# Four single PSUM tiles in place of two double ones in the joint keys of a packed attention and channel mix

## The chip, the cores and the metric

The kernel runs on one core of one Trainium2 chip. The metric is device time in microseconds (us), the median of several runs; lower is better. All profiles are of one execution on that core.

## What is computed

The reference is a two-step packed attention over eight batches, followed by a gated channel mix. Cut to what matters:

```python
p_packed = sm_attn(p, k, v)                # 32 packed rows per head
out      = sm_attn(q, p_packed, p_packed)  # (8, 8, 576, 64)
x        = out as (8, 576, 512)            # x_prev: x one row later, zeros first
xk = mu_k * x + (1 - mu_k) * x_prev
xr = mu_r * x + (1 - mu_r) * x_prev
k  = max(xk @ w_k, 0)                      # 512 -> 1024, the "keys"
v  = (k * k) @ w_v                         # 1024 -> 512, the "values"
r  = sigmoid(xr @ w_r)                     # 512 -> 512, the "gates"
return r * v
```

## The kernel before

The 4608 rows of the channel mix are cut into nine blocks of 512. Each fp32 product is made of three fp32r matmuls (high by high, high by low, low by high), so three matmuls of 128x128 by 128x512 form one step over a contraction of 128. The attention of later batches runs beside the channel mix of earlier blocks.

A planner written in the kernel (class `Flow`) runs generators, one for each piece of work, keeps the time at which each engine and each buffer slot should be free, and emits the instructions in the order in which it would start them. That order is fixed in the program: each engine takes its instructions in it, one after the other. Where an instruction needs what another engine makes, or overwrites what another engine still reads, the tile framework puts a semaphore wait on it. The framework keeps these dependences by tile.

The eight PSUM banks of 2 KB per partition are shared as follows. The tiles `m0` to `m3` have one bank each and serve keys, gates and values. The tiles `pa0` and `pa1`, made by `banks(slot)` (L276), have two banks each, shape 128 x 2 x 512, and serve attention.

The last two blocks (`PAIR` and `PAIR + 1`, blocks 7 and 8) have gates of their own (L1141 to L1143), and then their keys are made together (`keys_of_pair`, L1305 to L1341): seven products in place of eight, in the manner of Strassen and Winograd, each of two contraction steps of 128, so of six matmuls (all at L1334). There are two turns. In each turn a product is made for two column blocks `j` = 0 and 1 (`t` = 2 * turn + j). The order of the products is 1, 6, 7, 5, 2, 4, 3 in the first turn and 1, 6, 7, 5, 4, 3, 2 in the second. Products 1 and 6 open a `pa` tile for both `j`, products 7 and 5 open an `m` tile for each `j`; products 2, 4 and 3 add to the banks of 1, 7 and 5:

```python
FIRST_OF, WAITS = {2: 1, 4: 7, 3: 5}, {2: "u", 4: "x", 3: "c22"}
```

After each product a reader empties the bank: `first_of` copies product 1 to SBUF on ScalarE (ACT, L1355, result `c`, event `u`); `second_of` adds the bank of product 6 to it on VectorE (DVE, through `added`, L1195, event `v`); `third_of` adds product 7 (event `x`), `fourth_of` product 5 (`c22`), `low_left` product 4, `top_right` product 3, and `top_left` takes the relu of product 2 on ACT (L1385). Relu, square and the split into high and low follow (L1388 to L1426). `leave` gives a bank back to the planner, a double one after both its halves were read. Behind the joint keys come the values of the two blocks (L1170 to L1172), and then the gates' product with them (L1181) and the output's DMA (L242).

Of the kernel before, what the change touches and what calls it, by code (L numbers as in the profile page):

```python
# [8 lines left out]
F32 = mybir.dt.float32  # L9
# [173 lines left out]
def attn_pack_channel_mix(ctx: ExitStack, tc: tile.TileContext, q, k, v, p, mu_k, mu_r, w_k, w_v, w_r, out):  # L183
# [4 lines left out]
    P = 128  # L188
# [14 lines left out]
    flow = Flow()  # L203
# [33 lines left out]
    def pe(us, after=None):  # L237
        return "tensor", us, after, None
# [13 lines left out]
    def reached():  # L252
# [8 lines left out]
    sb = ctx.enter_context(tc.tile_pool(name="sb", bufs=1))  # L261
    dram = ctx.enter_context(tc.tile_pool(name="dram", bufs=1, space=bass.MemoryType.DRAM))
    ps = ctx.enter_context(tc.tile_pool(name="ps", bufs=1, space=bass.MemoryType.PSUM))
    BUFS = dict(raw=3, kq=4, vt=2, pt=1, a0=1, a1=1, aT=1, pm=2, e=2, a2=1, xt=4, tmp=4, xk=NC, sq=NF, sig=4,
                pa=2, both=1, m=4, staged=4, ex=7)
    for tag, n in BUFS.items():
        flow.pool(tag, n)
    flow.slots["m"].pop()
# [5 lines left out]
    MORE = {("sig", 4 + j): f"ex{3 + j}" for j in range(4)}  # L274

    def banks(slot):  # L276
        return ps.tile([P, 2, 512], F32, name="pa", tag=f"pa{slot}")

# [174 lines left out]
    def transposed_on_pe(tag, b, pr, raw_space, raw_slot, raw):  # L455

        yield from reached()
        kq = yield from flow.take("kq")
        t = tile_([P, S], F32, "kq", kq, tag)
        slot = yield from flow.take("pa")  # L460
        pT = banks(slot)
        yield pe(0.66)
        for hf in range(2):
            for c in range(3):
                nc.tensor.transpose(pT[:, hf, c * T6:(c + 1) * T6], raw[:T6, 3 * hf + c], ident[:T6, :T6])
        flow.give(raw_space, raw_slot)
        if b == 0 and pr < RANK_LATE14:
            done = flow.t
            yield vec(HS)
            nc.vector.tensor_copy(t[:, :HS], pT[:, 0, :HS])  # L470
            one = flow.t
            yield act(HS, after=done)
            nc.scalar.copy(t[:, HS:], pT[:, 1, :HS])
            flow.now.t = max(flow.t, one)
        else:
            yield act(S)
            nc.scalar.copy(t.rearrange("p (a b) -> p a b", a=2), pT[:, :, :HS])
        flow.give("pa", slot)
        ts[tag, b, pr] = kq, t
        flow.set((tag, b, pr))  # L480
# [68 lines left out]
    def first_side(h):  # L549
# [3 lines left out]
        slot = yield from flow.take("pa")  # L553
        yield pe(1.3)
        s1 = banks(slot)
        for hf in range(2):
            for j, half in enumerate(HALVES):
# [50 lines left out]
        slot = yield from flow.take("pa")  # L608
        yield pe(1.6)
        s2 = banks(slot).rearrange("p a b -> p (a b)")  # L610
        for k, (at, _) in enumerate(CHUNKS):
            for j in range(2):
# [690 lines left out]
    FIRST_OF, WAITS = {2: 1, 4: 7, 3: 5}, {2: "u", 4: "x", 3: "c22"}  # L1303

    def keys_of_pair():  # L1305
        left = [NF]
        for turn, order in enumerate(((1, 6, 7, 5, 2, 4, 3), (1, 6, 7, 5, 4, 3, 2))):
            opened, rooms = {}, {}
            for n in order:
                name, weights_ = PRODUCTS[n]  # L1310
                if n in (1, 6):
                    slot = yield from flow.take("pa")
                    both = banks(slot)
                    users = [2]
                for j in range(2):
                    t = 2 * turn + j
                    fs = slice(t * P, (t + 1) * P)
                    if n in (1, 6):
                        opened[n, j] = "pa", slot, both[:, j, :], users
                    elif n in (5, 7):  # L1320
                        one = yield from flow.take("m")
                        opened[n, j] = "m", one, ps.tile([P, 512], F32, name="ph", tag=f"m{one}"), [1]
                    more = n in FIRST_OF
                    bank = opened[FIRST_OF.get(n, n), j]
                    if more:
                        yield from flow.wait((WAITS[n], t))
                    for k in range(2):
                        yield from flow.wait(("difference", name, k), *([] if n in (1, 2, 4) else [("sum", {3: 4, 5: 1, 6: 2, 7: 3}[n], k)]))
                        yield pe(0.683)
                        flow.now.t -= flow.LAG  # L1330
                        wh, wl = weights_(k)
                        space, slot_, xh, xl = differences[name, k]
                        for step, (w, x) in enumerate(((wh, xh), (wh, xl), (wl, xh))):
                            nc.tensor.matmul(  # L1334
                                bank[2], w[:, fs], x, start=(not more and step == k == 0), stop=(step == 2 and k == 1),
                                skip_group_check=True,
                            )
                        if turn and j and space != "wk":
                            flow.give(space, slot_)
                    after = {1: first_of, 6: second_of, 7: third_of, 5: fourth_of, 2: top_left, 4: low_left, 3: top_right}[n]  # L1340
                    flow.spawn(after(turn, t, bank, rooms, left), 0, flow.t + flow.LAG)  # L1341

    def leave(bank):
        space, slot, _, users = bank
        users[0] -= 1
        if not users[0]:
            flow.give(space, slot)

    def first_of(turn, t, bank, rooms, left):
        space = "vt" if turn else "sq"  # L1350
# [7 lines left out]
    def second_of(turn, t, bank, rooms, left):  # L1358
        yield from flow.wait(("u", t))
        yield from added(rooms[t][1], rooms[t][1], bank[2])  # L1360
        leave(bank)
        flow.set(("v", t))
# [12 lines left out]
    def top_right(turn, t, bank, rooms, left):  # L1375
        yield from flow.wait(("c21", t))
        yield from added(rooms[t][1], rooms[t][1], bank[2])
        leave(bank)
        yield from later_square(t, rooms[t], rooms[t][1])

    def top_left(turn, t, bank, rooms, left):
        sr = yield from flow.take("tmp")
        r = tile_([P, WP], F32, "tmp", sr, "r")
        yield act(TB)
        nc.scalar.activation(r, bank[2], AF.Relu)  # L1385
        leave(bank)
        yield act(TB)
        nc.scalar.activation(r, r, AF.Square)  # L1388
        yield from squares_parted(PAIR, t, r, left)
        flow.give("tmp", sr)  # L1390
# [39 lines left out]
    def channel_mix():  # L1430
        for i in range(PAIR):
            yield from gates(i)
            yield from keys(i)
            if i + 1 < PAIR:
                mixes(i + 1)
            else:
                for h in range(2):
                    flow.spawn(mix(PAIR + h, 2, xrs, "xr"), 1 + 0.05 * h)
                flow.spawn(differences_of_keys(), 1.1)
            yield from values(i)  # L1440
        for h in range(2):
            yield from gates(PAIR + h)
        yield from keys_of_pair()
        for h in range(2):
            yield from values(PAIR + h, (0, 1, 4, 5, 6, 7, 2, 3))
# [91 lines left out]
```

## Time and profile before

| what | value |
|---|---|
| median of 3 runs | 587.63 us (587.18 to 588.07) |
| the profiled execution's own time | 586.58 us |
| its span, first to last instruction | 584.8 us |
| TensorE (PE) busy | 572.8 us, 98% of the span |
| VectorE (DVE) busy | 395.1 us, 68% |
| ScalarE (ACT) busy | 325.6 us, 56% |
| joint keys on PE | from 492.71 to 537.27 us |
| mean granted TensorE clock | 0.999 |

The busy time of PE counts overlapping matmuls once; two of them follow each other at a distance of some 0.23 us, and each is shown with 0.39 us. Idle time in a row stands in brackets with the instruction that ended it. So the cost of a gap is read from the distance between starts, and not from the bracket alone.

### The profile page before, as it was taken

How to read it: one execution, taken by the hardware profiler on the slowest of the kernel's cores; microseconds unless marked ns; L12 is line 12 of the kernel's file. 1: busy time of each engine (PE TensorE's matmuls, PEld its weight loads, DVE VectorE, ACT ScalarE, POOL GpSimd, SP SyncE). 2: the span in 40 equal slices, each digit the busy share in tenths (PEclk: the TensorE clock that was granted, in tenths of full speed). 3: DMA queues.
4: the chain of work that ended last, by engine and by line, in shares of the span. 5: the costliest groups of instructions: out<-in, count | busy, mean ns of one | idle time of the engine just before them, and what ended most of it. 6: DMA issues, size and time to landing. Idle time of an engine off the chain costs nothing.

```text
span 584.8 us, 9860 instructions
## 1 busy us (share of the span) xinstructions
PE 572.8 (98%) x3722; PEld 447.7 (77%) x3722; DVE 395.1 (68%) x745; ACT 325.6 (56%) x572; POOL 7.3 (1%) x36
## 2 busy tenths in 40 slices
PE   8999999999999999999999999999999999889997
PEld 7867777877777777777777777778888887667885
DVE  3797799739697688557953994479575992454531
ACT  3789979335576591665643764268456764346000
POOL 4000000000000000000000000000000000000000
PEclk9999999999999999999999999999999999999999
DMA  9899857646665542863375435000100010000011
GB/s 220 269 248 276 188 101 140 170 94 128 122 154 122 93 116 53 188 138 76 67 184 101 106 59 173 1 1 0 73 2 1 1 72 1 0 1 1 1 73 72
DMA packets 173823, 56.75 MB, mean 97 GB/s; under 512 B 150600, under 2 KB 164944, under 8 KB 173776
## 3 DMA queue, kind: packets, MB, share of 16 engines
q1 hardware_dynamic: 172928, 55.80, 40.5%
q8 instruction: 29, 0.48, 0.4%
q0 software_dynamic: 256, 0.26, 0.2%
q10 hardware_dynamic: 592, 0.07, 0.1%
q14 instruction: 18, 0.15, 0.1%
HBM read 43.13 MB, written 12.98 MB: 96 GB/s over the span
## 4 chain that ended last, share of the span: by engine, by line
PE 80%; DVE 7%; ACT 5%; DMA 4%; SPq 2%; issue 1%; POOL 0%; DVEq 0%; ACTq 0%; POOLq 0%
PE pvo L1170 10%; PE pvo L1171 9%; PE pvo L1172 9%; PE ph L1074 8%; PE ph L1076 7%; PE ph L1075 7%; PE pr L1141 5%; PE pr L1142 5%; PE pr L1143 5%; PE ph L1334 4%; PE pa L1334 3%; SPq L242 2%; DVE x L1041 2%; DMA st<-in_moe_w_r 2%; PE pa L914 2%; PE pa L742 1%
## 5 line engine op out<-in xcount | busy, mean ns | idle before, releaser
L1170 PE MATMUL pvo<-wv_h,sq 128*128 128x512 f32 x288 | 114.0, 396 | 0.2 <-ACT r L1086 0.2
L1171 PE MATMUL pvo<-wv_l,sq 128*128 128x512 f32 x288 | 112.2, 390 | 0.0
L1172 PE MATMUL pvo<-wv_h,sq 128*128 128x512 f32 x288 | 112.1, 389 | 0.0
L1074 PE MATMUL ph<-xk,wk_h 128*128 128x512 f32 x224 | 89.4, 399 | 0.0
L1075 PE MATMUL ph<-xk,wk_h 128*128 128x512 f32 x224 | 87.3, 390 | 0.0
L1076 PE MATMUL ph<-xk,wk_l 128*128 128x512 f32 x224 | 87.3, 390 | 0.0
L1170 PEld LDWEIGHTS pvo<-wv_h,sq 128*128 128x128 f32 x288 | 54.1, 188 | 17.9 <-issue 6.3
L1086 ACT ACTIVATE r<-ph 128x512 f32<-128x512 f32 x56 | 33.5, 598 | 61.2 <-PE ph L1076 57.8
L1172 PEld LDWEIGHTS pvo<-wv_h,sq 128*128 128x128 f32 x288 | 54.1, 188 | 11.4
L1171 PEld LDWEIGHTS pvo<-wv_l,sq 128*128 128x128 f32 x288 | 54.1, 188 | 10.6
L1041 DVE SCALAR_TENSOR_TENSOR x<-xt,mus,x 128x64 f32<-128x64 f32 (+7 forms) x117 | 52.7, 491 | 4.6 <-ACT x L1037 4.4
L1037 ACT ACTIVATE x<-xt,mus 128x64 f32<-128x64 f32 (+7 forms) x117 | 53.8, 514 | 1.2 <-DVE sq L1095 0.9
L1074 PEld LDWEIGHTS ph<-xk,wk_h 128*128 128x128 f32 x224 | 42.0, 188 | 13.1 <-issue 4.1
L1093 DVE CAST sq<-r 128x512 fp32r<-128x512 f32 x56 | 23.3, 417 | 42.4 <-ACT r L1089 41.1
L1141 PE MATMUL pr<-wr_h,xr 128*128 128x512 f32 x128 | 50.5, 395 | 0.0
L1142 PE MATMUL pr<-wr_l,xr 128*128 128x512 f32 x128 | 49.9, 390 | 0.0
L1143 PE MATMUL pr<-wr_h,xr 128*128 128x512 f32 x128 | 49.8, 389 | 0.0
L1076 PEld LDWEIGHTS ph<-xk,wk_l 128*128 128x128 f32 x224 | 42.0, 188 | 9.0
L1075 PEld LDWEIGHTS ph<-xk,wk_h 128*128 128x128 f32 x224 | 42.1, 188 | 8.0
L937 ACT COPY xt<-pa 128x576 f32<-128x576 f32 x28 | 33.3, 1254 | 14.2 <-PE pa L914 14.0
L1181 DVE TENSOR_TENSOR sig<-pvo,sig 128x512 f32<-128x512 f32 x36 | 23.3, 681 | 23.0 <-PE pvo L1172 22.9
L1095 DVE TENSOR_TENSOR sq<-r,sq 128x512 fp32r<-128x512 f32 x56 | 38.0, 679 | 1.0
(182 smaller groups left out, 849.7 us busy)
## 6 DMA issues: line engine op xcount, KB each, us to landing
out<-sig SPq DMA_DIRECT2D x36, 256.0 KB, 2.1
raw<-in_k SPq DMA_DIRECT2D x112, 72.0 KB, 2.7
raw<-in_q SPq DMA_DIRECT2D x112, 72.0 KB, 2.7
st<-in_moe_w_k SPq DMA_DIRECT2D x8, 512.0 KB, 5.8
st<-in_moe_w_v SPq DMA_DIRECT2D x8, 512.0 KB, 5.6
vt<-in_v SPq DMA_DIRECT2D x24, 160.0 KB, 3.4
away<-blocks SPq DMA_DIRECT2D x12, 288.0 KB, 2.7
vt<-in_v SPq DMA_DIRECT2D x24, 128.0 KB, 3.7
```

Source lines behind the costliest of these rows:

```text
L1037: nc.scalar.mul(x32[:, o:o + n], xts[b, c][:, 1 + s:1 + s + n], mus[:, j, c:c + 1])
L1041: nc.vector.scalar_tensor_tensor(x32[:, o:o + n], xts[b, c][:, s:s + n], mus[:, j + 1, c:c + 1], x32[:, o:o + n], op0=ALU.mult, op1=ALU.add,)
L1074: nc.tensor.matmul(ph, wk_h[:, c, fs], xh, start=(c == 0), stop=False)
L1075: nc.tensor.matmul(ph, wk_h[:, c, fs], xl, start=False, stop=False)
L1076: nc.tensor.matmul(ph, wk_l[:, c, fs], xh, start=False, stop=(c == NC - 1))
L1141: nc.tensor.matmul(pr, xh[:, ts_], wr_h[:, c, :], start=(c == 0), stop=False)
L1142: nc.tensor.matmul(pr, xh[:, ts_], wr_l[:, c, :], start=False, stop=False)
L1143: nc.tensor.matmul(pr, xl[:, ts_], wr_h[:, c, :], start=False, stop=(c == NC - 1))
L1170: nc.tensor.matmul(pv[t], sh, wv_h[:, f, :], start=(n == 0), stop=False)
L1171: nc.tensor.matmul(pv[t], sh, wv_l[:, f, :], start=False, stop=False)
L1172: nc.tensor.matmul(pv[t], sl, wv_h[:, f, :], start=False, stop=(n == NF - 1))
L1334: nc.tensor.matmul(bank[2], w[:, fs], x, start=(not more and step == k == 0), stop=(step == 2 and k == 1), skip_group_check=True,)
```

## The change

In `keys_of_pair` the four banks are taken one by one. The two `pa` tiles move to a pool of their own (`pp`), which is closed when the joint keys begin; a new pool (`late`) over the same four banks holds the tiles `n0` to `n3`, one bank each. Every product that opens a bank now opens one for its `j`, from slot kind `n` for products 1 and 6, and from `m` for 7 and 5, and `leave` gives back that bank alone.

```diff
+    pairs = ctx.enter_context(ExitStack())
+    pp = pairs.enter_context(tc.tile_pool(name="pp", bufs=1, space=bass.MemoryType.PSUM))
...
-                pa=2, both=1, m=4, staged=4, ex=7)
+                pa=2, both=1, m=4, n=4, staged=4, ex=7)
...
     def banks(slot):
-        return ps.tile([P, 2, 512], F32, name="pa", tag=f"pa{slot}")
+        return pp.tile([P, 2, 512], F32, name="pa", tag=f"pa{slot}")
...
     def keys_of_pair():
         left = [NF]
+        pairs.close()
+        late = ctx.enter_context(tc.tile_pool(name="late", bufs=1, space=bass.MemoryType.PSUM))
...
-                if n in (1, 6):
-                    slot = yield from flow.take("pa")
-                    both = banks(slot)
-                    users = [2]
                 for j in range(2):
                     t = 2 * turn + j
                     fs = slice(t * P, (t + 1) * P)
-                    if n in (1, 6):
-                        opened[n, j] = "pa", slot, both[:, j, :], users
-                    elif n in (5, 7):
-                        one = yield from flow.take("m")
-                        opened[n, j] = "m", one, ps.tile([P, 512], F32, name="ph", tag=f"m{one}"), [1]
+                    if n not in FIRST_OF:
+                        space = "m" if n in (5, 7) else "n"
+                        slot = yield from flow.take(space)
+                        opened[n, j] = space, slot, (ps if space == "m" else late).tile(
+                            [P, 512], F32, name="ph", tag=f"{space}{slot}"
+                        )
...
     def leave(bank):
-        space, slot, _, users = bank
-        users[0] -= 1
-        if not users[0]:
-            flow.give(space, slot)
+        flow.give(*bank[:2])
```

Every engine has the same instructions in the same order as before, by operation and operands; what changes is the tiles that L1334 (now L1335) writes, and the waits on its matmuls. In the rows below a number is part of a tile's name, and a wait names the engine whose semaphore is awaited.

On PE, the first turn, product 1 (moving tile `dB11`) and the start of product 6 (`dT2`), before:

```order
L1334 MATMUL pa_5319<-dB11_5185,wk_l_127 128x512
L1334 MATMUL pa_5319<-dB11_5000,wk_h_126 128x512 x2
L1334 MATMUL pa_5319<-dB11_5000,wk_l_127 128x512
L1334 MATMUL pa_5319<-dB11_5185,wk_h_126 128x512 [waits Activation_49]
L1334 MATMUL pa_5319<-dB11_5185,wk_h_126 128x512
L1334 MATMUL pa_5319<-dB11_5185,wk_l_127 128x512
L1334 MATMUL pa_5336<-dT2_5092,s2_4733 128x512 [waits PE_49]
L1334 MATMUL pa_5336<-dT2_5092,s2_4733 128x512
L1334 MATMUL pa_5336<-dT2_5092,s2_4734 128x512
L1334 MATMUL pa_5336<-dT2_5263,s2_4839 128x512
L1334 MATMUL pa_5336<-dT2_5263,s2_4839 128x512 [waits DVE_49]
```

The same place in the changed kernel:

```order
L1335 MATMUL ph_5326<-dB11_5188,wk_l_130 128x512
L1335 MATMUL ph_5335<-dB11_5003,wk_h_129 128x512 x2
L1335 MATMUL ph_5335<-dB11_5003,wk_l_130 128x512
L1335 MATMUL ph_5335<-dB11_5188,wk_h_129 128x512 x2
L1335 MATMUL ph_5335<-dB11_5188,wk_l_130 128x512
L1335 MATMUL ph_5344<-dT2_5095,s2_4736 128x512 x2
L1335 MATMUL ph_5344<-dT2_5095,s2_4737 128x512
L1335 MATMUL ph_5344<-dT2_5266,s2_4842 128x512 [waits Activation_49]
L1335 MATMUL ph_5344<-dT2_5266,s2_4842 128x512 [waits DVE_49]
L1335 MATMUL ph_5344<-dT2_5266,s2_4843 128x512
```

Before, the second half of product 1 (`j` = 1) is in the tile of the first half, and its second step waits for ACT. In the changed kernel it has a tile of its own and no wait; a wait on ACT stands at product 6 instead, on the matmul that first takes the second half of `dT2`.

On PE, the second turn, the end of product 6 and the start of product 7 (`dT3`), before:

```order
L1334 MATMUL pa_5471<-dT2_5092,s2_4733 128x512 x2
L1334 MATMUL pa_5471<-dT2_5092,s2_4734 128x512
L1334 MATMUL pa_5471<-dT2_5263,s2_4839 128x512 [waits DVE_49]
L1334 MATMUL pa_5471<-dT2_5263,s2_4839 128x512
L1334 MATMUL pa_5471<-dT2_5263,s2_4840 128x512
L1334 MATMUL ph_5487<-dT3_5051,s3_4714 128x512 x2
L1334 MATMUL ph_5487<-dT3_5051,s3_4715 128x512
```

The same place in the changed kernel:

```order
L1335 MATMUL ph_5490<-dT2_5095,s2_4736 128x512 [waits Activation_49]
L1335 MATMUL ph_5490<-dT2_5095,s2_4736 128x512
L1335 MATMUL ph_5490<-dT2_5095,s2_4737 128x512
L1335 MATMUL ph_5490<-dT2_5266,s2_4842 128x512 x2
L1335 MATMUL ph_5490<-dT2_5266,s2_4842 128x512
L1335 MATMUL ph_5498<-dT3_5054,s3_4717 128x512 [waits DVE_49]
L1335 MATMUL ph_5498<-dT3_5054,s3_4717 128x512
```

The wait on DVE in the middle of the second half of product 6 is gone. The first matmul into each bank that is opened again has a wait on the reader of what the bank held: ACT for product 6, whose bank held product 2, and DVE for product 7, whose bank held product 4.

On PE, the first turn, the end of product 2 (`dB21`) and the start of product 4 (`dT4`), before:

```order
L1334 MATMUL pa_5319<-dB21_5184,wk_h_126 128x512 x2
L1334 MATMUL pa_5319<-dB21_5184,wk_l_127 128x512
L1334 MATMUL pa_5319<-dB21_5264,wk_h_126 128x512 [waits Activation_49]
L1334 MATMUL pa_5319<-dB21_5264,wk_h_126 128x512
L1334 MATMUL pa_5319<-dB21_5264,wk_l_127 128x512
L1334 MATMUL ph_5351<-dT4_5198,wk_h_126 128x512 [waits DVE_49]
```

The same place in the changed kernel:

```order
L1335 MATMUL ph_5335<-dB21_5187,wk_h_129 128x512 [waits Activation_49]
L1335 MATMUL ph_5335<-dB21_5187,wk_h_129 128x512
L1335 MATMUL ph_5335<-dB21_5187,wk_l_130 128x512
L1335 MATMUL ph_5335<-dB21_5267,wk_h_129 128x512 x2
L1335 MATMUL ph_5335<-dB21_5267,wk_l_130 128x512
L1335 MATMUL ph_5360<-dT4_5201,wk_h_129 128x512 [waits DVE_49]
```

The wait on ACT stood in the middle of the second half's six matmuls; in the changed kernel it stands at their start, on the copy of product 1 out of this bank.

## Rows read from the trace of the kernel before

**Rows 1.** The page: busy time by engine, and the granted clock in 40 slices.
```profile
PE 572.8 (98%) x3722; PEld 447.7 (77%) x3722; DVE 395.1 (68%) x745; ACT 325.6 (56%) x572; POOL 7.3 (1%) x36
...
PEclk9999999999999999999999999999999999999999
```

**Rows 2.** Waits of PE over the whole span: us in total, times, longest us.
```profile
PE pa L1334 <- DVE c L1195: 1.7, 2, 0.9
...
PE pa L1334 <- ACT r L1385: 1.4, 2, 0.7
PE pa L1334 <- ACT c L1355: 1.4, 2, 0.7
```

**Rows 3.** The chain in order of time, joint keys: start, us, engine, tile, line.
```profile
494.95 0.59 ACT c L1355
...
498.71 0.70 DVE c L1195
...
500.42 5.45 PE ph L1334 x24
...
507.99 0.61 ACT r L1385
...
517.20 0.59 ACT c L1355
...
520.97 0.70 DVE c L1195
...
535.82 0.60 ACT r L1385
```

**Rows 4.** Timeline of PE at gaps: start, us, line, operation, tiles, [idle before].
```profile
494.52 0.39 PE L1334 MATMUL pa<-dB,wk_l 128*128 128x512 f32 x1
495.59 0.73 PE L1334 MATMUL pa<-dB,wk_h 128*128 128x512 f32 x2 [0.68 <-ACT c L1355]
496.16 0.40 PE L1334 MATMUL pa<-dB,wk_l 128*128 128x512 f32 x1
496.39 2.21 PE L1334 MATMUL pa<-dT,s 128*128 128x512 f32 x9
499.45 0.73 PE L1334 MATMUL pa<-dT,s 128*128 128x512 f32 x2 [0.85 <-DVE c L1195]
...
500.26 0.85 PE L1334 MATMUL ph<-dT,s 128*128 128x512 f32 x3
...
535.39 0.39 PE L1334 MATMUL pa<-dB,wk_l 128*128 128x512 f32 x1
536.47 0.72 PE L1334 MATMUL pa<-dB,wk_h 128*128 128x512 f32 x2 [0.69 <-ACT r L1385]
...
537.27 0.40 PE L1170 MATMUL pvo<-wv_h,sq 128*128 128x512 f32 x1
```

**Rows 5.** Windows: length, busy time (instructions) of PE, PEld, DVE, ACT, POOL; clock; DMA.
```profile
508.64:517.84 9.20, 8.52 (x36) 6.68 (x36) 6.78 (x12) 7.16 (x13) 0.00 (x0) 1.00 0.00 0
...
492.71:537.27 44.56, 40.14 (x170) 31.07 (x169) 18.78 (x30) 20.96 (x35) 0.00 (x0) 1.00 0.00 1
```

**Rows 6.** Tile pa from 400 us: the last instructions of attention that read it.
```profile
L937 ACT COPY xt<-pa x4: 1227/1237/1298, 405.6 to 410.8; 128x576 f32<-128x576 f32 x4
```

**Rows 7.** Timeline of DVE and PE: readers of banks, and products 4 and 3.
```profile
501.83 0.69 DVE L1195 TENSOR_TENSOR c<-c,ph 128x512 f32<-128x512 f32 x1 [0.61 <-PE ph L1334]
...
524.11 0.69 DVE L1195 TENSOR_TENSOR c<-c,ph 128x512 f32<-128x512 f32 x1 [0.63 <-PE ph L1334]
...
526.84 0.69 DVE L1195 TENSOR_TENSOR c<-c,ph 128x512 f32<-128x512 f32 x1 [0.67 <-PE ph L1334]
...
533.74 0.69 DVE L1195 TENSOR_TENSOR c<-c,ph 128x512 f32<-128x512 f32 x1
...
528.00 0.63 PE L1334 MATMUL ph<-dT,wk_h 128*128 128x512 f32 x2
...
530.80 2.90 PE L1334 MATMUL ph<-dB,s 128*128 128x512 f32 x12
```

## The prediction

> **What bounds the kernel now.** I read the page first: TensorE (PE) is busy 98% of the span, at full clock in every slice [rows 1]. So time can only come from work taken off PE or from gaps in its stream. Next I read PE's waits over the whole span: three of the four largest entries, two waits each, belong to L1334, the joint keys of the last two blocks: for a VectorE (DVE) add at L1195, a ScalarE (ACT) relu at L1385 and an ACT copy at L1355 [rows 2]. Then the chain of work that ended last, in order of time: inside the joint keys it leaves PE six times, for those same readers, and returns to PE each time [rows 3]. Six such detours, and each lies on the chain that sets the end: what is saved there is saved from the kernel's time, unless something else takes over. Last I read PE's timeline at the gaps, to price them [rows 4].
>
> **Why PE waits.** Look at the first gap. The row at 494.52 is the third matmul of `j` = 1 in product 1, so the last one of `j` = 0 began three steps earlier, at 493.84, and was over at 494.23. The copy of `j` = 0 starts only at 494.95, right after the matmul of 494.52 is over (494.52 + 0.39 = 494.91) [rows 3, 4]. Then PE waits until that copy is over and resumes at 495.59. Both halves lie in different banks, but in one tile: the copy waits for what was written to the other half, and the next matmul into the other half waits for the copy. The wait that PE has there is the one on ACT that stands in the middle of the second half's six matmuls. The contrast is in the same stage: products 7 and 5 have a tile for each `j`, their readers are DVE adds too, and 24 matmuls of theirs run through without a gap in 5.45 us, 0.227 us apart [rows 3]; the add that reads product 7 begins at 501.83 while PE goes on [rows 7].
>
> **What the change takes away.** With a tile for each `j`, neither half waits for the other. Price of one gap, from start to start, against 0.227 a step [rows 4]:
> - ACT kind: from 494.52 to 496.16 are three steps, 0.68, and it took 1.64: 0.96 lost. At the end of the second turn, from 535.39 to 537.27 are four steps, 0.91, and it took 1.88: 0.97. There are four of this kind (copies of product 1 and relus of product 2, two turns); the two not shown there have the same idle time within 0.01.
> - DVE kind (product 6, two turns): nine matmuls begin at 496.39 and take 2.21, so the ninth begins at 496.39 + 2.21 - 0.39 = 498.21; the next product begins at 500.26, four steps (0.91) later by plan and 2.05 in fact: 1.14 lost. The second turn's has the same detour in the chain [rows 3].
> Sum: 4 x 0.96 + 2 x 1.14 = 6.1 us.
>
> The bracket alone would give less: 4 x 0.69 + 2 x 0.85 = 4.5 us [rows 4]. It counts from the end of the matmul before, though matmuls overlap, and misses that after a gap the second matmul follows 0.34 us behind the first and not 0.23. The upper bound is the whole stage against an even pace: 44.56 us for 168 matmuls [rows 5], and 168 x 0.227 = 38.1, so 6.4 us. I take 6.1, which lies between, because starts are what the rest of the stream is moved by.
>
> **What it adds.** No instruction is added or moved on any engine; the planner's order is the same. New are waits on PE for the true reader of each bank. I price them by their cover, the time from the reader's end to the matmul that needs it:
> - The first matmul of the stage now follows the closing of attention's pool. Attention's last read of those banks begins at 410.8 [rows 6], over 80 us earlier: nothing.
> - Least cover of all: in the second turn product 4 starts at 528.00 and needs the add that starts at 524.11 and takes 0.69, and product 3 starts at 530.80 and needs the one from 526.84: 3.2 and 3.3 us [rows 7]. No gap lies between these pairs, so this cover stays. In the first turn product 4 needs the add of 501.83, over at 502.52; it comes 36 steps and one gap after 500.26, at 509.4, and without that gap at 508.4: 5.9 us are left.
> - Banks opened again in the second turn were read 8 us or more before, by a replay of the stage with the durations of its rows: nothing.
> - The values behind the keys need the four `m` banks. Their last reader in the stage starts at 533.74, so is over at 534.43; the values begin at 537.27 [rows 4, 7] and need the fourth bank three steps of three matmuls later. They move up by one gap: cover 1.9 us for the first bank, even if it were the last one freed, and 3.9 for the fourth.
> - ACT and DVE have the same work in less time. In the stretch from 508.64 to 517.84 ACT is busy 7.16 of 9.20 us and DVE 6.78 [rows 5]; one gap less leaves 8.24 us. Tight, but enough, and ACT's copies at the head of the second turn aren't needed before product 6's adds.
>
> One rule speaks against single tiles. In rows: 24 matmuls into four single tiles, with four endings that a DVE add waits for, keep the step of 0.227 us [rows 3], so an ending costs PE nothing that I can see. The Trainium skill ("TensorE: Matmul & The Clock Gate", section "The cost: per-tile semaphore tail") says that increments at the end of each tile's matmul serialize, with some 26 ns for each. As an estimate by that page, the twelve group endings of products 1, 6 and 2 would cost 0.3 us, and the gain would be 5.8 us; the trace does not agree.
>
> And one would raise the gain. In rows: the granted clock is 1.00 over the whole stage, gaps and all [rows 5], and the steps after a gap are as short as before it, so no clock is lost now and none can be given back. The Trainium skill (same page, section "A second HAM failure mode: psum-queue depth-cycling") tells of kernels whose short idle times between groups of matmuls made the clock swing; no gap here does that.
>
> **The sum.** Profiled execution 586.58 - 6.1 = 580.5 us (its span 584.8 becomes 578.7). It lay 1.05 us under the median of the runs shown, so the median goes from 587.63 to 581.5. The values and the end run as before, only earlier: they hang on PE alone.
>
> **The rivals.**
> 1. *Only a part goes.* The two DVE gaps of product 6 might stay under another name, since the add there also needs the copy of product 1. For it: DVE is the later of the two in the chain, 0.70 against 0.59 [rows 3]. Against: in the new order the second half of product 6 has no wait on an add, and the copy is over before product 6 ends. Then only 4 x 0.96 = 3.8 go: 583.8 us.
> 2. *Nothing changes.* The framework could still guard the new pool's four tiles as one region, or the values could wait for squares for as long as they come earlier. Against the first: the waits in the middle of second halves are gone from the order of PE. Against the second: the values take products of the first turn first. 587.6 us.
> 3. *Slower: ACT falls behind.* At the change of turns ACT has 7.16 us of work in 8.24. If its reads of PSUM took longer beside denser matmuls, the copies of product 1 in the second turn would slip, and behind them the adds of products 6 and 7 and then product 4 on PE. A slip of D costs PE D - 3.2 us, so the time is 581.5 + D - 3.2, and the kernel is slower than before from D = 9.3 us on. For that ACT's 7.16 us would have to become 7.16 + 1.08 + 9.3 = 17.5, about 2.4 times as long; at three times (21.5 us, D = 13.3) the kernel would take 591.6 us. Against it: reading PSUM beside running matmuls costs DVE nothing now, 0.69 us at 501.83 against 0.70 at 498.71, in a gap [rows 3, 7], and ACT's copies and relus at the gaps take 0.59 to 0.61 us.
>
> **How the numbers follow.** My forecast has 0.89, rival 1 0.06, rival 2 0.03, rival 3 0.02. A change of 0.2%, 1.2 us, is about what a measurement of this kernel can tell from none. The forecast and rival 1 are both faster by more: 0.95 in all; rival 2 is the 0.03 within 0.2%; rival 3 is the 0.02 slower. The range: the bounds of the gain, 4.5 to 6.4, give 581.2 to 583.1; the runs before lay within 0.45 of their median, so 580.8 at the low end, and at the high end rival 1 at 583.8 is taken in.
>
> **What would show it.** If I am right, PE's timeline in the joint keys has no gap of over 0.1 us at a wait for ACT or DVE, the stage takes 38.2 to 38.6 us instead of 44.56, the copy of product 1 starts about 0.7 us earlier after the stage's first matmul (some 1.6 us instead of 2.24), the chain of work stays on PE from the gates to the end of the values, and the time before the stage is unchanged. I am wrong if a wait for DVE is left at product 6, if a new idle row stands before product 4, 3 or 7 or before the first values, or if the step between matmuls rises over 0.235 us.

## The result and the profile after

The changed kernel takes 581.06 us in the median of 4 runs (580.74 to 583.50) against 587.61 us before (587.18 to 588.07): ratio 0.9897, 95% interval 0.987 to 0.9925 (ratios here and below go by the means of the runs, and the one run of 583.50 us raises this one; that of the medians is 0.9888). The median is 6.55 us lower, where 6.1 were forecast; the time lies 0.4 us under the forecast of 581.5, inside the range, and the change is clear of 0.2%.

Read the profile after in the order in which the one before was read. First the page: the span is now 579.3 us, and PE's busy time has hardly moved, so its share went from 98% [rows 1] to 99%.

```profile
PE 571.4 (99%) x3722; PEld 448.6 (77%) x3722; DVE 395.3 (68%) x745; ACT 325.0 (56%) x572; POOL 7.3 (1%) x36
```

Next, PE's waits over the whole span (us in total, times, longest). The three entries of the joint keys [rows 2] are gone; what is left are waits in the start, in attention, and a short one in the values of an earlier block (L1172).

```profile
PE spare L1506 <- POOL ident masks.py:199: 1.6, 1, 1.6
PE pa L962 <- DVE xr L975: 0.8, 1, 0.8
PE pa L765 <- DVE pm L759: 0.6, 1, 0.6
PE pa L807 <- ACT a L793: 0.3, 1, 0.3
PE pa L916 <- DVE m L902: 0.3, 1, 0.3
PE pvo L1172 <- ACT r L1088: 0.2, 1, 0.2
```

Then the chain in order of time (start, us, engine, tile, line). Before, it left PE six times in the joint keys [rows 3]; now the whole stage is one piece of 168 matmuls.

```profile
493.64 38.37 PE ph L1335 x168
```

And PE's timeline at the place of the first gap [rows 4]: the second half of product 1 starts at 494.83, its second step at 495.51, 0.22 us behind the matmul before it, and no row has idle time in brackets. Product 6 runs straight into product 7 in the row of 15 matmuls.

```profile
494.61 0.39 PE L1335 MATMUL ph<-dB,wk_l 128*128 128x512 f32 x1
494.83 0.62 PE L1335 MATMUL ph<-dB,wk_h 128*128 128x512 f32 x2
495.29 0.39 PE L1335 MATMUL ph<-dB,wk_l 128*128 128x512 f32 x1
495.51 0.62 PE L1335 MATMUL ph<-dB,wk_h 128*128 128x512 f32 x2
495.97 0.39 PE L1335 MATMUL ph<-dB,wk_l 128*128 128x512 f32 x1
496.19 3.56 PE L1335 MATMUL ph<-dT,s 128*128 128x512 f32 x15
```

The windows view of the stage (length; busy time and instructions of PE, PEld, DVE, ACT, POOL; clock; DMA) says the same in one row: 38.38 us, and PE busy for all of it, where it was 40.14 of 44.56 us [rows 5].

```profile
493.47:531.85 38.38, 38.38 (x170) 31.54 (x168) 18.74 (x30) 20.50 (x35) 0.00 (x0) 1.00 0.00 1
```

The readers now work beside the matmuls. In ACT's timeline the two copies of product 1 are below, in DVE's the first add of product 6 and the add that product 4 of the second turn waits for, and in PE's that product 4.

```profile
495.03 0.59 ACT L1353 COPY c<-ph 128x512 f32<-128x512 f32 x1 [0.76 <-PE ph L1335]
496.39 0.59 ACT L1353 COPY c<-ph 128x512 f32<-128x512 f32 x1 [0.77 <-PE ph L1335]
...
497.82 0.69 DVE L1197 TENSOR_TENSOR c<-c,ph 128x512 f32<-128x512 f32 x1 [7.76 <-PE ph L1335]
...
519.66 0.69 DVE L1197 TENSOR_TENSOR c<-c,ph 128x512 f32<-128x512 f32 x1 [0.60 <-PE ph L1335]
...
523.54 0.63 PE L1335 MATMUL ph<-dT,wk_h 128*128 128x512 f32 x2
```

The first copy starts 495.03 - 493.47 = 1.56 us behind the stage's first matmul, where it was 2.24; its half ended at 494.61 + 0.39 = 495.00. It no longer waits for the other half.

In the second turn it still does. In PE's and ACT's timelines, the first and the last matmul of the first half of product 1, the third of the second half, and the copy of the first half:

```profile
512.66 0.62 PE L1335 MATMUL ph<-dB,wk_h 128*128 128x512 f32 x2
...
513.79 0.39 PE L1335 MATMUL ph<-dB,wk_l 128*128 128x512 f32 x1
...
514.47 0.39 PE L1335 MATMUL ph<-dB,wk_l 128*128 128x512 f32 x1
...
514.90 0.59 ACT L1353 COPY c<-ph 128x512 f32<-128x512 f32 x1 [0.68 <-PE ph L1335]
```

The first half is over at 513.79 + 0.39 = 514.18. But in the trace none of its matmuls increments PE's semaphore, for which the copy waits; the next one that does is the third of the second half, over at 514.47 + 0.39 = 514.86. So this copy starts 514.90 - 512.66 = 2.24 us behind the product's first matmul, as the first copy did before, and yet PE has no gap, since the second half does not wait for the copy. What costs time is PE's wait for the reader, and not the reader's wait for the other half.

### The profile page after: what moved, and what is told of

It reads as the page before. It is cut to its first block, busy times and chain, and to the rows that moved or that the text cites. A ratio compares the mean times of both kernels' runs of the same rounds, so it can differ in the third digit from the quotient of the medians.

```text
span 579.3 us, 9860 instructions
## 1 busy us (share of the span) xinstructions
PE 571.4 (99%) x3722; PEld 448.6 (77%) x3722; DVE 395.3 (68%) x745; ACT 325.0 (56%) x572; POOL 7.3 (1%) x36
## 4 chain that ended last, share of the span: by engine, by line
PE 81%; DVE 7%; ACT 5%; DMA 4%; SPq 2%; issue 1%; POOL 0%; DVEq 0%; ACTq 0%; POOLq 0%
PE pvo L1172 10%; PE pvo L1173 10%; PE pvo L1174 10%; PE ph L1076 8%; PE ph L1077 8%; PE ph L1078 8%; PE ph L1335 7%; PE pr L1143 5%; PE pr L1144 5%; PE pr L1145 5%; DVE x L1043 2%; PE pa L916 2%; SPq L242 2%; DMA st<-in_moe_w_r 2%; PE pa L744 1%; PE pa L720 1%
## 5 line engine op out<-in xcount | busy, mean ns | idle before, releaser
L1172 PE MATMUL pvo<-wv_h,sq 128*128 128x512 f32 x288 | 114.0, 396 | 0.2 <-ACT r L1088 0.2
L1172 PEld LDWEIGHTS pvo<-wv_h,sq 128*128 128x128 f32 x288 | 54.1, 188 | 17.9 <-issue 6.3
L1154 ACT ACTIVATE sig<-pr 128x512 f32<-128x512 f32 x36 | 21.2, 600 | 31.3 <-PE pr L1145 31.2
```

The source lines that it names most:

```text
L1172: nc.tensor.matmul(pv[t], sh, wv_h[:, f, :], start=(n == 0), stop=False)
```

## The experiments

My theory (A): the gaps come from dependences that are kept by tile. Rivals: (B) the single banks gain because each comes free by itself; (C) the gain lies in the new pools and the place of their banks. Two sets of runs, each with the kernel before on the same chip: median 586.95 us in the first (14 runs; up to the swapped tiles), 586.97 us in the second (9 runs; the last three). The stage's length below is always from the first matmul of the joint keys to the first of the values, in the profiled execution of that run.

**The changed kernel once more**, without an edit.

> The changed kernel once more, on the same chip as the next three. All theories: 581.1 us, 6.5 us under the kernel before; no gap on PE in the joint keys.

580.80 us, ratio 0.9898 (0.9883 to 0.9913), so 6.15 us faster; stage 493.06 to 531.43, 38.37 us, in one piece. As expected.

**Double tiles, readers after both halves.** The kernel before, with three lines changed in `keys_of_pair`: the readers of a product are collected and go into the program once both halves' matmuls are in it. Waits of the framework follow the order of the program.

```diff
+                readers = []
                 for j in range(2):
...
-                    flow.spawn(after(turn, t, bank, rooms, left), 0, flow.t + flow.LAG)
+                    readers.append(after(turn, t, bank, rooms, left))
+                for reader in readers:
+                    flow.spawn(reader, 0, flow.t + flow.LAG)
```

> The kernel before, with its double tiles, but the readers of a product are put into the program only after the matmuls of both halves. Theory A (gaps come from dependences kept by tile: a reader that stands between the halves ties the second half to it): no reader stands between matmuls into its tile any more, so all six gaps go although the tiles stay double; joint keys 38.4 us, time 581.1 to 581.6. Theory B (the single banks gain by coming free one by one): double tiles still come free in pairs, so the gaps stay: 587.6. Theory C (the new pool and the place of its banks): nothing of it is here, 587.6.

580.56 us, ratio 0.9894 (0.9879 to 0.9909): all of the gain, with the old pools and the old double tiles. The chain in order of time goes through the stage without leaving PE:

```profile
493.18 5.44 PE pa L1335 x24
498.62 5.44 PE ph L1335 x24
504.06 2.77 PE pa L1335 x12
506.84 5.53 PE ph L1335 x24
512.37 5.44 PE pa L1335 x24
517.81 10.97 PE ph L1335 x48
528.78 2.77 PE pa L1335 x12
```

The stage takes 38.37 us (493.02 to 531.39). The copies now both run behind the second half, the first of them 2.92 us behind the stage's first matmul where it is 1.56 in the changed kernel, and PE has no gap behind them:

```profile
495.94 1.08 ACT L1358 COPY c<-pa 128x512 f32<-128x512 f32 x2 [2.12 <-PE pa L1335]
```

This is the run that decides against B and C: banks still come free in pairs, and no pool is new.

**Only the pools.** Attention's pool is closed and a late pool opened, as in the change, but products 1 and 6 take double tiles in it.

```diff
-                    both = banks(slot)
+                    both = late.tile([P, 2, 512], F32, name="pa", tag=f"n{slot}")
```

> Only the pools of the change: attention's pool is closed and a late pool opened, but products 1 and 6 still take double tiles there. Theory A: the six gaps stay, 587.6 us, joint keys 44.6 us. Theory B: 587.6 as well. Theory C: the gain comes from here, 581.1.

586.98 us, ratio 1.0001 (0.9992 to 1.001): no difference that can be measured. The stage takes 44.54 us (493.72 to 538.26), and the chain leaves PE six times as before; its first four pieces:

```profile
493.89 2.05 PE pa L1338 x9
495.96 0.59 ACT c L1359
496.60 3.03 PE pa L1338 x12
499.73 0.70 DVE c L1197
```

So closing the pool and the place of the banks bring nothing.

**Tiles swapped.** In the kernel before, products 7 and 5 (and 4 and 3 on their banks) get the double tiles, and 1 and 6 (and 2) the single ones.

```diff
-                if n in (1, 6):
+                if n in (5, 7):
                     slot = yield from flow.take("pa")
...
-                    if n in (1, 6):
+                    if n in (5, 7):
                         opened[n, j] = "pa", slot, both[:, j, :], users
-                    elif n in (5, 7):
+                    elif n in (1, 6):
```

> The kernel before with the tiles swapped: products 1 and 6 (and 2, on 1's bank) in single tiles, products 7 and 5 (and 4 and 3, on their banks) in double ones. Theory A: the six gaps go, and eight new ones come, each behind a DVE add, at products 7, 5, 4 and 3 in both turns: 8 x 1.14 = 9.1 us or more where DVE is behind, so joint keys of 47.5 us or more and 590.2 us or more. Theories B and C: the banks that come free in pairs are needed again only in the next turn, so no gap is expected: between 581 and 587.6.

589.15 us, ratio 1.004 (1.0026 to 1.0055): slower than before, as only A has it, but by 2.2 us and not 2.6 or more. PE's waits name eight gaps, all behind L1195, and none behind ACT:

```profile
PE pa L1334 <- DVE c L1195: 4.7, 6, 0.8
...
PE pa L1334 <- DVE r L1195: 1.6, 2, 0.8
```

The stage takes 46.83 us (492.76 to 539.59), 8.46 over 38.37: 1.06 us for each gap, not 1.14. The idle rows show where the difference lies:

```profile
501.18 0.50 PE L1334 MATMUL pa<-wk_h,s 128*128 128x512 f32 x1 [0.78 <-DVE c L1195]
...
511.56 0.74 PE L1334 MATMUL pa<-dT,wk_h 128*128 128x512 f32 x2 [0.78 <-DVE r L1195]
```

0.78 us idle, where product 6 had 0.85 [rows 4]. The 47.5 us or more that were expected for the stage were 0.7 us too high, eight times the 0.08 us by which each gap is smaller.

**Product 1 alone in single tiles**, product 6 double; and **product 6 alone in single tiles**, product 1 double (the same edit with the two numbers exchanged). Both use the late pool.

```diff
-                pa=2, both=1, m=4, n=4, staged=4, ex=7)
+                pa=2, both=1, m=4, n=2, d=1, staged=4, ex=7)
...
+                if n == 6:
+                    slot = yield from flow.take("d")
+                    both = late.tile([P, 2, 512], F32, name="pa", tag=f"d{slot}")
...
+                    if n == 6:
+                        opened[n, j] = "d", slot, both[:, j, :], users
+                    elif n == 1:
+                        one = yield from flow.take("n")
+                        opened[n, j] = "n", one, late.tile([P, 512], F32, name="ph", tag=f"n{one}"), [1]
```

> Late pool; product 1 (with 2 on its bank) in two single tiles, product 6 in one double tile. Theory A: the four ACT gaps go, 4 x 0.96 = 3.8 us, and the two DVE gaps stay: 583.7 us, joint keys 40.7 us. Theory B or C: all of the gain or none, 581 or 587.6.

583.12 us, ratio 0.9933 (0.9916 to 0.9949). The stage takes 40.66 us (494.17 to 534.83). PE's waits in the stage:

```profile
PE pa L1341 <- DVE c L1197: 1.7, 2, 0.8
```

> Late pool; product 6 in two single tiles, product 1 (with 2 on its bank) in one double tile. Theory A: the two DVE gaps go, 2 x 1.14 = 2.3 us, and the four ACT gaps stay: 585.3 us, joint keys 42.2 us.

584.93 us, ratio 0.996 (0.9947 to 0.9972). The stage takes 42.26 us (493.91 to 536.17). PE's waits in the stage:

```profile
PE pa L1341 <- ACT r L1392: 1.4, 2, 0.7
PE pa L1341 <- ACT c L1362: 1.4, 2, 0.7
```

Each kind of gap goes with its own tile and takes its own price along. Against the 38.37 us without gaps, two DVE gaps cost 40.66 - 38.37 = 2.29 us, 1.15 each, and four ACT gaps 42.26 - 38.37 = 3.89 us, 0.97 each. Together that is 6.18, which is what the whole change takes from the stage (44.56 - 38.38): the prices add up. In time the two runs are 3.85 and 2.04 us under the kernel before, where 3.8 and 2.3 were expected.

**Single tiles given back in pairs.** In the changed kernel `leave` collects the slots of a pair and gives both back after the second.

```diff
-        flow.give(*bank[:2])
+        if bank[0] == "m":
+            flow.give(*bank[:2])
+            return
+        pair = gone.setdefault(bank[1] // 2, [])
+        pair.append(bank[1])
+        if len(pair) == 2:
+            for slot in gone.pop(bank[1] // 2):
+                flow.give("n", slot)
```

> The changed kernel, but the planner gets the single banks of products 1 and 6 back only in pairs. Theory A: the tiles are what counts, nothing waits for a bank: 581.1 us. Theory B: the banks come free late, the gain goes: up to 587.6 us.

580.96 us, ratio 0.9893 (0.9877 to 0.9908); stage 38.37 us (493.59 to 531.96). The program that comes out has the same order and the same waits as the changed kernel's, so this is a third timing of it. What it shows is that the planner holds nothing back when the banks come back only in pairs: giving them back late moves not one instruction. B has nothing to stand on here.

## Why the prediction was right

- *The cause.* The gaps were named as dependences kept by tile. Shown: they go with double tiles kept, once no reader stands between the halves in the program; they stay with the new pools alone; and they follow the double tiles to other products.
- *The price.* 4 x 0.96 + 2 x 1.14 = 6.1 us was forecast from start to start; the parts measured alone give 0.97 and 1.15, and the stage became 6.18 us shorter, 38.38 us in the forecast's window of 38.2 to 38.6. The sum of the idle times in brackets, 4.5 us, would have been 1.7 too low: what a gap costs includes the overlap that is lost.
- *The covers.* The least one was put at 3.2 us, before product 4 of the second turn. After: the add is over at 519.66 + 0.69 = 520.35 and product 4 starts at 523.54, so 3.19. No wait that was added cost PE anything. ACT's copies take 0.59 us beside running matmuls, as they did in a gap, so rival 3 has no part of it.
- *The rules weighed.* The granted clock of the stage is 1.00 before and after, so none was given back. The increments at tile ends were rightly put at nothing, but not for the whole reason: the change adds none. In the traces 28 of the stage's 168 matmuls increment PE's semaphore, before as after; only the places of some move. With the readers after both halves there are 22, and the stage takes the same 38.37 us as in the repeat of the changed kernel with its 28, so an increment has no price here that can be seen. The Trainium skill ("TensorE: Matmul & The Clock Gate", section "The cost: per-tile semaphore tail") has some 26 ns for each, from which the estimate of 5.8 us was worked out. The runs do not agree: the stage gained 6.18.
- *Rivals 1 and 2.* No gap stayed at product 6, and the values start 0.23 us behind the last key, so nothing was lost again there.
- *What was off.* I wrote that the time before the stage would be unchanged. In the profiled execution of the changed kernel the stage starts at 493.47 and not at 492.71, 0.76 us later, so that the two spans differ by only 5.5 us where the stage gained 6.18. The program ahead of the stage has the same order and waits; what is known of this is in the last section. The medians differ by 6.55, 0.37 more than the stage gained and 0.45 more than was forecast. The kernel before alone differs by 0.66 between this set of runs (587.61) and the next (586.95), and no run ties the 0.4 to the change; in the repeat the gain was 6.15.

## What to carry to other kernels

When PE waits in the middle of an accumulation, ask which reader it waits for, and whether that reader reads another half of the same tile: where dependences are kept by tile, as here, a tile that spans two PSUM banks lets each half wait for the other half's readers, and each reader for the other half's matmuls. The first costs PE time; the second by itself cost nothing here. Either one tile for each bank, or readers that come into the program only after all writes to the tile, takes the wait away; both gave the same time here. Price such a gap from start to start of the matmuls, and before you drop a wait look for the next true reader of the bank and how long its work has been over.

## What was not expected

*A gap behind the same add has two sizes.* Behind product 6 it is 0.85 us idle and 1.15 in all; behind products 7, 5, 4 and 3, in the run with swapped tiles, 0.78 and 1.06. In the rows, the add of product 6 starts later behind PE. In the kernel before, the nine matmuls of the second turn's product 6 end at 518.65 + 2.21 = 520.86 and the add starts at 520.97, 0.11 us behind; in the run with swapped tiles the add of product 7 starts 0.04 us behind its matmuls (499.56 + 0.84 = 500.40). These are the rows:

```profile
518.65 2.21 PE L1334 MATMUL pa<-dT,s 128*128 128x512 f32 x9
...
520.97 0.69 DVE L1195 TENSOR_TENSOR c<-c,pa 128x512 f32<-128x512 f32 x1 [4.05 <-PE pa L1334]
```

```profile
499.56 0.84 PE L1334 MATMUL pa<-dT,s 128*128 128x512 f32 x3
...
500.44 0.69 DVE L1195 TENSOR_TENSOR c<-c,pa 128x512 f32<-128x512 f32 x1 [1.28 <-PE pa L1334]
```

The add of product 6 waits for two other engines, PE and the ACT copy of product 1; those of the other products wait for PE and at most for DVE's own earlier add. That may be the 0.07 us; no run tells it apart.

*The start is not the same in each execution.* The joint keys begin between 492.71 us (the kernel before) and 494.17 us (product 1 alone in single tiles) though all that is ahead of them is the same. The latest have waits of PE for loads in the first stage that the kernel before does not have among its waits. In the run with product 1 alone:

```profile
PE pv L581 <- DMA vt<-in_v: 1.8, 1, 1.8
```

With the pools alone that wait has 1.6 us and the stage begins at 493.72; in the profile with swapped tiles there is none and it begins at 492.76. So up to some 1.5 us of what one execution shows against another lie ahead of the stage, and in the latest ones most of that stands beside a wait for a load.

The profile of the changed kernel itself, which is 0.76 us late, has no such wait in its list. Its stream on PE is 0.6 us behind by 20 us from the start, and one wait in attention is 0.8 us, in the list above, where the kernel before has 0.5:

```profile
PE pa L960 <- DVE xr L973: 0.5, 1, 0.5
```

What made it late stays open. Either way, a change of a microsecond is better read from its own stage than from two spans.
